# Attention with two pairs of heads as a couple: the last 64 queries of both scored on four quarters of TensorE

## The chip, the cores and the metric

The kernel runs on one core of a Trainium2 chip. The metric is the device time of one execution in microseconds; before the change the median of three runs is 960.37 us (960.06 to 960.45). Less is better.

## What is computed

Three stages follow each other. The first is causal attention with a gated memory read, the other two are chains of matrix products:

```python
# 4 batches, 8 heads, 576 positions, 64 features a head
scores = q @ k.T / 8; scores = where(causal, -1e9, scores)
a = exp(scores - scores.max(-1)); a /= a.sum(-1) + 1e-9
local = a @ v
q_p = where(q > 0, q, exp(q) - 1) + 1
mem = (q_p @ M_prev) / (q_p . z_prev + 1e-6)
x = g * mem + (1 - g) * local            # g = sigmoid(beta), a number per head
# 2304 tokens of 512 features
x = ((x @ w1) * (x @ w2)) @ w3 @ w_out   # w1, w2: 512 x 1024; w3: 1024 x 1024
h = x @ w_in                             # 512 x 2048
out = (h - tanh(h)) @ moe2_w_out         # 2048 x 512
```

## The kernel before

**The whole.** `block_kernel` runs the attention (to about 220 us, with its last products later), then for six groups of 384 tokens the product of two projections (`ab_pe`, line 846, and `x2_pe`, line 872, to about 550 us), then the tanh stage (`h2_pe`, line 1020, `out_pe`, line 1077). The product w3 @ w_out is formed once by the kernel itself, beside the attention: `fold_pe` (line 303) is a generator of 64 pieces of three matmuls (tile `fo`) that the attention loop takes a few at a time. Weights come as raw 64-bit words and are decoded on chip by `decode` (line 260): for each 128 x 512 block two operations on GpSimd (tiles `T`, `E`), two on ScalarE (`T`, `E`), one on VectorE, then a split in a high part on GpSimd and a low part on VectorE. Names in the trace are tile names: `sc` scores, `st` row maxima and sums, `p` exponentials, `t` transposes in PSUM, `g` transposes copied to SBUF, `o` products with V in PSUM, `xs` the attention result, `r` the q and k of a pair, `v` its V, `mw` and `mo` the memory part, `raw` encoded weights. Every instruction goes through one wrapper, so all have line 50.

**Attention.** Heads are taken two at a time: 16 pairs, four to a batch. A pair's q and k lie in one tile `r`, the first head on partitions 0 to 63, the second on 64 to 127. The 576 queries are blocks u = 0 to 3 of 128 and u = 4 of 64. `GROUPS` (line 390) makes four lots of them: (0, 1), (2), (3), (4); so there are 64 steps m, and the loop at line 770 takes two steps in a round, two rounds to a pair. For a full block, `scores` (line 399) puts the first 64 queries of a head in partitions 0 to 63 of the PSUM tile and the others in 64 to 127, and the two heads in two banks: four matmuls of 64 rows by 64 columns, each with up to 512 moving columns, on the four quarters of the array. For the block of 64 queries the partitions hold the two heads, and 576 keys are cut in two halves of 288, so that only the two quarters on the diagonal are used at a time:

```python
            if us[0][0] == 4:
                for x in range(2):
                    for h, r in hr:
                        y = x ^ h
                        mm(sc[r, y, 0:288], q[r, 512:576], k[r, 288 * y:288 * y + 288], True, y == 0)
```

A bf16 product of `identb` and `maskb` adds the causal mask. Score tiles have two PSUM buffers, transposes two, products two.

**A round.** On each engine the instructions of the attention run in program order (`Ordered`, with `in_order` set). A round at even m does: for the two lots of the round before `recip` (VectorE: reciprocals of the row sums) and `norm` (GpSimd: scaling of `p`); `scores` and `rmax` (VectorE: row maxima) of steps m and m + 1; `work(m)`, that is the background work of the step (`background`, line 710: decoding, memory part) and `exps(m)` (ScalarE); `av` (line 504: one product with V of the pair before, copied out by ScalarE as `xs`); `pieces` of the fold; `trans` (line 473) of the first lot of the round before (TensorE transposes, copied to `g` by ScalarE and VectorE); `work(m + 1)`; more `pieces`; `trans` of the second lot. In the first nine steps `background` comes after `exps` (`SHORT`). `load_qk`, `load_v` and the raw loads are issued from SP; `r` has three buffers, V two, `raw` three. `scale_q` (line 212) multiplies the q of the next pair by 0.125 on ScalarE; it stands at the end of a pair's first round, behind all else.

**After the attention** the order of instructions of the other stages is left to the compiler's scheduler, which also moves the first `ab` products in among the last rounds of the attention.

Of the kernel before, what the change touches and what calls it, by code (L numbers as in the profile page):

```python
# [33 lines left out]
def block_kernel(ctx, tc, qk, qt, vt, mp, zp_d, beta, w1, w2, w3t, wo, wi, wo2, ident_d, mask_d, out):  # L34
# [138 lines left out]
    def tp(o, i):  # L173
# [7 lines left out]
    PIECES = (1, 2, 0, 2)  # L181
# [11 lines left out]
        ("r", RB), ("1", 1), ("2", 2), ("4", 4), ("z", ZB), ("t", TB))]  # L193
# [58 lines left out]
    jobs, todo, raws, live = [], deque(fold_seq), [], [0]  # L252
# [7 lines left out]
    def decode(item):  # L260
        k, raw, dst = item
        late = lambda: fstep[0] >= SHORT
        rb = raw[:].bitcast(U32).rearrange("p (n t) -> p n t", t=2)
        lw, hw = rb[:, :, 0], rb[:, :, 1].bitcast(F32)
        t = apt.tile([128, 512], U32, tag="T", name="T")
# [3 lines left out]
        e = ap2.tile([128, 512], U32, tag="E", name="E")  # L269
# [22 lines left out]
        DV.tensor_tensor(out=lo, in0=tf, in1=hi.bitcast(F32), op=ALU.subtract)  # L292
        if k[0] in range(8):
            folds.append((k, fstep[0]))
# [37 lines left out]
    if True:  # L332
# [57 lines left out]
        GROUPS = ((0, 1), (2,), (3,), (4,))  # L390
        NM = 16 * len(GROUPS)
# [3 lines left out]
        def step(m):  # L395
            P, s = divmod(m, len(GROUPS))
            return P, [(u, 128 * x) for x, u in enumerate(GROUPS[s])]

        def scores(m):
            P, us = step(m)  # L400
            q, k = qk_t[P][:, 0], qk_t[P][:, 1]
            hr = [(h, slice(64 * h, 64 * h + 64)) for h in range(2)]
            sc = sc_t[m] = pss.tile([128, 2, 512], F32, tag="sc", name="sc")
            qs = [(h, r, y, slice(64 * y, 64 * y + 64)) for y in range(2) for h, r in hr]
            for u, a in us:
                if u == 4:
                    continue
# [5 lines left out]
            if us[0][0] == 4:  # L413
                for x in range(2):
# [17 lines left out]
        def exps(m):  # L432
            P, us = step(m)
            st = st_t[m]
            for x, (u, a) in enumerate(us):
                sc = seen(m, u, a)
                p = p_t[P, u] = ap3.tile([128, PW[u]], F32, tag=f"p{u}", name="p")
                p = p[:].rearrange("p (a n) -> p a n", a=2)
# [34 lines left out]
        def trans(P, u):  # L473
            p = p_t.pop((P, u))
            if u == 0:
                g_t[0] = ap2.tile([128, 2, 2, 256], F32, tag="g0", name="g0")
            if u == 2:
                g_t[1] = ap1.tile([128, 4, 2, 320], F32, tag="g1", name="g1")
                g_t[2] = ap1.tile([64, 2, 64], F32, tag="g2", name="g2")
            if u < 4:  # L480
                K = 128 * u + 128
                blocks = [(kb, h) for kb in range(u + 1) for h in range(2)]
                for c in range(0, len(blocks), 4):
# [4 lines left out]
                    G = g_t[0] if u < 2 else g_t[1]  # L488
# [15 lines left out]
        def av(P, grp):  # L504
# [4 lines left out]
            hr = [(h, slice(64 * h, 64 * h + 64)) for h in range(2)]  # L509
# [4 lines left out]
            else:  # L514
                for kb in range(4):
                    q0 = 128 if kb == 3 else 0
                    for h, r in hr:
                        mm(o[r, q0:320], v[:, kb, h], g_t[1][:, kb, h, q0:320], kb == 0, False)
                for h, r in hr:
                    mm(o[r, 256:320], v[0:64, 4, h], g_t[2][:, h], False, True)  # L520
            ch = b * 9 + grp * 4
            finished[0] = 2 * P + grp + 1
# [184 lines left out]
        coming, begun, active, owed = [0], [0], [0], [0]  # L707
        ahead()

        def background(m):  # L710
# [13 lines left out]
            if m >= coming[0] and begun[0] < len(fold_seq) and active[0] < TB:  # L724
# [15 lines left out]
        load_qk(1)  # L740
# [19 lines left out]
        def work(h):  # L760
# [5 lines left out]
            if h < SHORT:  # L766
                background(h)

        m = 0
        while m < NM + 3 or jobs or late or folded[0] < 16 or begun[0] < len(fold_seq):  # L770
            P, s = divmod(m, 4)
            fstep[0] = m
            if 2 <= m <= NM:
                for h in (m - 2, m - 1):
                    recip(h)
                for h in (m - 2, m - 1):
                    norm(h)
            if m < NM:
                fill(FILL["s"].get(m, 0))
                for h in (m, m + 1):  # L780
                    if h == 1:
                        first_q(320, 576)
                    scores(h)
# [3 lines left out]
                if m == 2:  # L787
# [7 lines left out]
            trs = 0 <= m - WAIT < NM  # L795
            pieces(m, PIECES[s])
            if trs:
                fill(FILL["t"].get(m, 0))
                for u in GROUPS[(m - WAIT) % 4]:
                    trans((m - WAIT) // 4, u)  # L800
# [4 lines left out]
            if trs:  # L805
                for u in GROUPS[(m + 1 - WAIT) % 4]:
                    trans((m + 1 - WAIT) // 4, u)
# [383 lines left out]
```

## Time and profile before

| | |
|---|---|
| median of three runs | 960.37 us |
| the profiled execution | 960.0 us, of which the span of instructions is 958.2 us |
| TensorE matmul busy | 942.0 us (98%) |
| TensorE weight load busy | 815.6 us (85%) |
| VectorE | 677.5 us (71%) |
| ScalarE | 621.8 us (65%) |
| GpSimd | 407.0 us (42%) |
| chain that ended last | TensorE 90%, VectorE 6%, ScalarE 2% |

Busy times are unions of the recorded intervals, so overlapping matmuls are not counted twice; the difference of 1.8 us between the execution and its span lies before the first and after the last instruction. An fp32 matmul stands as two records, so that eight `sc` records are four matmuls. The page's averages mix three stages; the change is in the first of them.

### The profile page before, as it was taken

The numbers are of one execution on the slowest core, as the hardware profiler recorded it, in microseconds if no ns is written. First come the engines' busy times: TensorE is split into PE (matmuls) and PEld (weight loads), VectorE is DVE, ScalarE is ACT, GpSimd is POOL, SyncE is SP. The second block draws the span as 40 slices with busy tenths as digits, with TensorE's granted clock in tenths as the row PEclk, the third lists the DMA queues.
The fourth block names the chain that finished last, engine by engine and source line by source line (L and its number), as shares of the span: only waits on it lengthen the run. The fifth ranks groups of instructions, "written<-read, shape, count | busy, mean of one in ns | idle before, by whom it ended". The sixth has DMA issues, their size and how long they took to land.

```text
span 958.2 us, 16304 instructions
## 1 busy us (share of the span) xinstructions
PE 942.0 (98%) x5927; PEld 815.6 (85%) x5928; DVE 677.5 (71%) x1185; ACT 621.8 (65%) x1398; POOL 407.0 (42%) x500
## 2 busy tenths in 40 slices
PE   7999999999999999999999999999999999999998
PEld 3566665668989999999999999999999998999996
DVE  6788877995876653534424678887787888887875
ACT  6788886875456542324526687776777867766864
POOL 5778866884665511202308753222222222222222
PEclk9999999999999999999999999999999999999999
DMA  6454544341445520101501100000000000000000
GB/s 231 174 174 157 187 145 161 120 138 45 143 130 185 170 69 31 55 12 67 155 1 44 45 1 1 1 34 1 20 14 1 34 1 1 34 1 1 34 1 34
DMA packets 26080, 68.29 MB, mean 71 GB/s; under 512 B 4880, under 2 KB 5904, under 8 KB 26000
## 3 DMA queue, kind: packets, MB, share of 16 engines
q1 hardware_dynamic: 25568, 67.12, 21.3%
q8 instruction: 46, 0.75, 0.3%
q14 instruction: 34, 0.28, 0.1%
q10 hardware_dynamic: 432, 0.14, 0.1%
HBM read 62.53 MB, written 4.72 MB: 70 GB/s over the span
## 4 chain that ended last, share of the span: by engine, by line
PE 90%; DVE 6%; ACT 2%; issue 1%; DMA 1%; POOL 1%; SPq 0%; DVEq 0%; ACTq 0%; POOLq 0%
PE o L50 25%; PE h L50 21%; PE ab L50 20%; PE x L50 11%; PE sc L50 4%; PE t L50 4%; PE fo L50 4%; DVE st L50 2%; PE mo L50 2%; ACT p L50 1%; DVE g L50 1%; DVE T L50 1%; DVE mst L50 0%; POOL p L50 0%; DMA r<-in_qk 0%
## 5 line engine op out<-in xcount | busy, mean ns | idle before, releaser
L50 POOL TENSOR_TENSOR gl<-s,gh 128x384 fp32r<-128x384 f32 x96 | 99.7, 1038 | 288.3 <-ACT gh L50 275.8
L50 PE MATMUL x<-abh,wf 128*128 128x384 f32 x384 | 107.0, 342 | 1.1 <-ACT abh L50 1.1
L50 ACT ACTIVATE s<-u,pc 128x384 f32<-128x384 f32 x192 | 107.7, 614 | 0.6 <-POOL gl L50 0.6
L50 PE MATMUL ab<-xh,wa 128*128 128x384 f32 x384 | 106.9, 338 | 0.7 <-ACT xh L50 0.6
L50 PE MATMUL ab<-xh,wb 128*128 128x384 f32 x384 | 106.0, 336 | 0.0
L50 DVE SCALAR_TENSOR_TENSOR s<-s,u 128x384 f32<-128x384 f32 x96 | 84.3, 878 | 25.7 <-ACT s L50 24.9
L50 POOL TENSOR_SCALAR p<-p,st 128x128 f32<-128x128 f32 (+2 forms) x144 | 86.0, 616 | 36.4 <-DVE st L50 26.8
L50 ACT ACTIVATE p<-sc,st 128x128 f32<-128x128 f32 (+2 forms) x144 | 78.1, 555 | 29.2 <-DVE st L50 28.3
L50 ACT ACTIVATE u<-u,pc 128x384 f32<-128x384 f32 x96 | 59.4, 619 | 47.1 <-DVE s L50 47.1
L50 DVE TENSOR_TENSOR a<-ab,a 128x384 f32<-128x384 f32 x48 | 26.4, 552 | 73.1 <-PE ab L50 69.7
L50 PEld LDWEIGHTS x<-abh,wf 128*128 128x128 f32 x384 | 70.2, 188 | 5.6 <-issue 3.9
L50 DVE TENSOR_TENSOR t<-h,t 128x384 f32<-128x384 f32 x96 | 53.2, 554 | 28.8 <-ACT t L50 28.3
L50 POOL TENSOR_SCALAR T<-raw 128x512 f32<-128x512 f32 x72 | 56.6, 787 | 39.1 <-DMA raw<-in_wo 11.5
L50 ACT ACTIVATE u<-h 128x384 f32<-128x384 f32 x96 | 46.7, 487 | 40.7 <-PE h L50 40.7
L50 PEld LDWEIGHTS ab<-xh,wa 128*128 128x128 f32 x384 | 70.1, 188 | 2.1 <-ACT xh L50 0.9
L50 POOL TENSOR_SCALAR E<-raw 128x512 f32<-128x512 f32 x72 | 51.1, 710 | 47.2 <-DVE z2p L50 12.8
L50 PEld LDWEIGHTS ab<-xh,wb 128*128 128x128 f32 x384 | 70.0, 188 | 0.3 <-issue 0.3
L50 DVE SCALAR_TENSOR_TENSOR s<-s,s 128x384 f32<-128x384 f32 x96 | 63.9, 665 | 8.7 <-DVE s L50 0.5
L50 PE MATMUL sc<-r 64*64 64x128 f32 (+4 forms) x640 | 64.8, 455 | 0.6 <-DVE r L50 0.6
L50 DVE COPY_PREDICATED s<-u,t 128x384 f32<-128x384 uint32 x96 | 58.7, 612 | 8.9 <-DVE s L50 0.5
L50 PE MATMUL x<-abl,wf 128*128 128x384 f32 x192 | 64.9, 338 | 0.0
L50 ACT ACTIVATE E<-raw 128x512 uint16<-128x512 uint32 x72 | 57.3, 796 | 11.5 <-POOL E L50 11.2
(208 smaller groups left out, 2514.4 us busy)
## 6 DMA issues: line engine op xcount, KB each, us to landing
raw<-in_wo SPq DMA_DIRECT2D x24, 512.0 KB, 3.5
r<-in_qk SPq DMA_DIRECT2D x15, 576.0 KB, 5.1
raw<-in_w3t SPq DMA_DIRECT2D x16, 512.0 KB, 3.8
raw<-in_w SPq DMA_DIRECT2D x16, 512.0 KB, 3.5
raw<-in_wi SPq DMA_DIRECT2D x16, 512.0 KB, 3.6
v<-in_vt SPq DMA_DIRECT2D x16, 320.0 KB, 2.9
mw<-in_qt SPq DMA_DIRECT2D x18, 256.0 KB, 3.8
out<-ob SPq DMA_DIRECT2D x18, 256.0 KB, 2.2
```

Of the source, the lines that this page charges most:

```text
L50: i = call(*args, **kw)
```

## The change

The pairs are taken two at a time (a couple, 2b and 2b + 1), in four rounds of two steps: (0, 1) and (2) of the first pair; (3) of the first and (0, 1) of the second; (2) and (3) of the second; and the last 64 queries of both. In this last round a PSUM tile holds one head, its partitions the two pairs, so that four matmuls of 288 columns run on the four quarters, and both tiles are filled alternately. Each round has one product with V. What was done to both score tiles, exponentials and transposes of the last 64 queries is done as often as before, but each transpose tile is now copied out in two halves, one by ScalarE and one by VectorE, since its halves belong to two pairs. The tile `g1` exists once for each pair of the couple and holds the last 64 keys as well (the tile `g2` goes); `g0`, one of the `E` tiles and two of the four `T` tiles of the decoding are given up or taken from another pool. Each pair's q and k are loaded at the end of the couple's last round, two pairs at a time; pair 1 is loaded before the first raw weights; V is loaded one round before its first use. `scale_q` stands in the middle of the first and third round, between the transposes of the first lot and `work(m + 1)`. In the first nine steps `background` of an even step comes after the transposes of the first lot. `recip`, `norm` and `trans` take the two lots in the same order; in a couple's first round that is the second lot first. The exponentials of a `u = 4` of a second head use the buffer of `p2`.

```diff
-    PIECES = (1, 2, 0, 2)
+    PIECES = (1, 2, 0, 2, 1, 2, 0, 2)
...
-        GROUPS = ((0, 1), (2,), (3,), (4,))
-        NM = 16 * len(GROUPS)
+        SEQ = ((0, (0, 1)), (0, (2,)), (0, (3,)), (1, (0, 1)), (1, (2,)), (1, (3,)), (0, (4,)), (1, (4,)))
+        NM = 64
...
+        def scores_last(m):
+            P, us = step(m)
+            sc = [pss.tile([128, 2, 512], F32, tag="sc", name="sc") for _ in hr]
+            sc_t[m], sc_t[m + 1] = sc
+            for y in range(2):
+                for j, c in hr:
+                    q, k = qk_t[P + j][:, 0], qk_t[P + j][:, 1]
                     for h, r in hr:
-                        y = x ^ h
-                        mm(sc[r, y, 0:288], q[r, 512:576], k[r, 288 * y:288 * y + 288], True, y == 0)
+                        mm(sc[h][c, y, 0:288], q[r, 512:576], k[r, 288 * y:288 * y + 288], True, y == 0)
+            for j, c in hr:
                 for h, r in hr:
-                    mm(sc[r, 1, 224:288], identb[r, r], maskb[r, 0:64], False, True)
+                    mm(sc[h][c, 1, 224:288], identb[r, r], maskb[r, 0:64], False, True)
...
             else:
+                h = P % 2
                 t = psT.tile([128, 4, 128], F32, tag="t", name="t")
                 for kb in range(4):
                     tp(t[:, kb], p[:, 128 * kb:128 * kb + 128])
-                copy(g_t[1][:].rearrange("p a b q -> p (a b) q")[:, :, 256:320],
-                     t[:].rearrange("p a (b q) -> p (a b) q", b=2))
+                for j in range(2):
+                    copy(g_t[1, j][:, :, h, 256:320], t[:, :, 64 * j:64 * j + 64], on_act=j == 0)
                 t = psT.tile([128, 4, 128], F32, tag="t", name="t")
                 tp(t[0:64, 0], p[:, 512:576])
-                copy(g_t[2][:], t[0:64, 0].rearrange("p (b q) -> p b q", b=2), on_act=False)
+                for j in range(2):
+                    copy(g_t[1, j][0:64, 3, h, 0:64], t[0:64, 0, 64 * j:64 * j + 64], on_act=j == 0)
...
+        load_qk(1)
         ahead()
...
+            lots = (m - 2, m - 1) if s else (m - 1, m - 2)
...
+                if s == 6:
+                    scores_last(m)
...
                 if m == 0:
                     set_gates()
-                if m == 2:
                     first_q(0, 576, 1)
             work(m)
             flush_t()
-            if 1 <= P <= 16:
-                av(P - 1, s // 2)
-                if s == 2 and P + 1 < 16:
-                    load_v(P + 1)
+            if s == 0 and 1 <= b <= 8:
+                av(2 * b - 1, 0)
+            if s == 2 and 1 <= b <= 8:
+                av(2 * b - 2, 1)
+                if b < 8:
+                    load_v(2 * b)
+            if s == 4 and b < 8:
+                av(2 * b, 0)
+            if (s == 6 and 1 <= b < 8) or (s == 4 and b == 8):
+                av(2 * b - 1, 1)
+                if b < 8:
+                    load_v(2 * b + 1)
...
+                lot(lots[0])
+            if m < SHORT:
+                background(m)
+            if s == 0 and 1 <= b < 8:
+                scale_q(2 * b + 1)
+            if s == 4 and b < 7:
+                scale_q(2 * b + 2)
             work(m + 1)
...
+                lot(lots[1])
...
-            if s == 0 and 1 <= P <= 16 - RB:
-                load_qk(P + RB - 1)
-            if s == 0 and 1 <= P < 15:
-                scale_q(P + 1)
+            if s == 6:
+                for P in (2 * b + 3, 2 * b + 4):
+                    if P < 16:
+                        load_qk(P)
```

## Rows read from the trace of the kernel before

**Rows 1.** Stretches: length, busy us of PE, PEld, DVE, ACT, POOL, clock, DMA, GB/s.

```profile
0.00:42.00 42.00, 35.20 (x297) 17.62 (x299) 28.53 (x62) 29.07 (x83) 26.86 (x50) 0.96 0.58 201
42.00:215.00 173.00, 170.28 (x1617) 111.93 (x1618) 147.13 (x311) 143.87 (x393) 133.36 (x195) 1.00 0.48 157
...
180.00:200.00 20.00, 19.89 (x183) 13.04 (x177) 19.79 (x37) 16.19 (x48) 17.79 (x23) 1.00 0.38 136
```

**Rows 2.** TensorE, one pair of the middle: start, duration, operation, records.

```profile
129.21 1.09 PE L50 MATMUL sc<-r 64*64 64x512 f32 x8
...
130.17 1.16 PE L50 MATMUL sc<-r 64*64 64x288 f32 x8
...
131.29 2.42 PE L50 MATMUL o<-g,v 128*64 128x320 f32 x20
...
136.51 0.45 PE L50 MATMUL sc<-r 64*64 64x128 f32 x8
...
137.31 0.84 PE L50 MATMUL sc<-r 64*64 64x384 f32 x8
...
138.12 0.87 PE L50 MATMUL o<-g,v 128*64 128x256 f32 x8
138.92 0.97 PE L50 MATMUL fo<-wa,zs 128*128 128x512 f32 x3
139.74 1.03 PE L50 MATMUL t<-ident,p 128*128 128x128 f32 x8
140.53 0.95 PE L50 MATMUL fo<-wb,zs 128*128 128x512 f32 x3
...
142.01 0.71 PE L50 MATMUL t<-ident,p 128*128 128x128 f32 x5
```

**Rows 3.** ScalarE in the same pair; in brackets idle before, and releaser.

```profile
130.43 0.73 ACT L50 ACTIVATE r<-r 128x576 f32<-128x576 f32 x1
131.01 0.68 ACT L50 ACTIVATE T<-T 128x512 f32<-128x512 f32 x1
131.79 0.69 ACT L50 ACTIVATE p<-sc,st 128x512 f32<-128x512 f32 x1
...
138.73 0.37 ACT L50 ACTIVATE p<-sc,st 128x128 f32<-128x128 f32 x1 [1.16 <-DVE st L50]
...
140.33 0.48 ACT L50 ACTIVATE xs<-o,omgt 128x256 f32<-128x256 f32 x1
140.69 0.61 ACT L50 ACTIVATE g<-t 128x512 f32<-128x512 f32 x1
141.17 0.82 ACT L50 ACTIVATE E<-raw 128x512 uint16<-128x512 uint32 x1
141.80 0.60 ACT L50 ACTIVATE p<-sc,st 128x384 f32<-128x384 f32 x1
...
142.35 0.62 ACT L50 ACTIVATE p<-sc,st 128x384 f32<-128x384 f32 x1
```

**Rows 4.** VectorE in the same pair: the row maxima of its second round.

```profile
137.62 1.89 DVE L50 TENSOR_REDUCE st<-sc 128x2 f32<-128x256 f32 x3
```

**Rows 5.** Opening: the first raw loads, GpSimd's first decode, TensorE after a wait.

```profile
2.75 1.55 SPq L50 DMA_DIRECT2D raw<-in_wo  x3
...
9.36 0.64 POOL L50 TENSOR_SCALAR T<-raw 128x512 f32<-128x512 f32 x1 [8.43 <-DMA raw<-in_wo]
...
22.79 0.84 PE L50 MATMUL t<-ident,p 128*128 128x128 f32 x5 [1.62 <-ACT g L50]
23.57 1.98 PE L50 MATMUL sc<-r 64*64 64x512 f32 x8
...
25.42 1.79 PE L50 MATMUL sc<-r 64*64 64x288 f32 x8
```

**Rows 6.** DMA issues from 42 to 215 us: count, size, median us to landing.

```profile
r<-in_qk SPq DMA_DIRECT2D x11, 576.0 KB, 5.1
v<-in_vt SPq DMA_DIRECT2D x13, 320.0 KB, 2.9
```

More of the change, by code (lines that the diff above doesn't have):

```diff
@@ L251, in block_kernel @@
     folds, fstep, folded, fold_open = deque(), [0], [0], [False]
-    jobs, todo, raws, live = [], deque(fold_seq), [], [0]
+    jobs, todo, raws, live, turn, going = [], deque(fold_seq), [], [0], [0], set()
     def ahead():
@@ L264, in decode @@
         lw, hw = rb[:, :, 0], rb[:, :, 1].bitcast(F32)
-        t = apt.tile([128, 512], U32, tag="T", name="T")
+        n = turn[0]
+        turn[0] += 1
+        going.add(n)
+        t = (stg["T"] if n & 2 else apt).tile([128, 512], U32, tag="T", name="T")
         tf = t[:].bitcast(F32)
@@ L268, in decode @@
         yield 0, 0, 0.7
-        e = ap2.tile([128, 512], U32, tag="E", name="E")
+        e = (stg["E"] if n & 1 else ap1).tile([128, 512], U32, tag="E", name="E")
         PO.tensor_scalar(out=e[:].bitcast(F32), in0=hw, scalar1=2.0 ** -100, scalar2=2.0 ** -53,
@@ L292, in decode @@
         DV.tensor_tensor(out=lo, in0=tf, in1=hi.bitcast(F32), op=ALU.subtract)
+        going.discard(n)
         if k[0] in range(8):
@@ L395, in step @@
         def step(m):
-            P, s = divmod(m, len(GROUPS))
-            return P, [(u, 128 * x) for x, u in enumerate(GROUPS[s])]
+            b, s = divmod(m, 8)
+            j, us = SEQ[s]
+            return 2 * b + j, [(u, 128 * x) for x, u in enumerate(us)]
+        hr = [(h, slice(64 * h, 64 * h + 64)) for h in range(2)]
         def scores(m):
@@ L401, in scores @@
             q, k = qk_t[P][:, 0], qk_t[P][:, 1]
-            hr = [(h, slice(64 * h, 64 * h + 64)) for h in range(2)]
             sc = sc_t[m] = pss.tile([128, 2, 512], F32, tag="sc", name="sc")
@@ L436, in exps @@
                 sc = seen(m, u, a)
-                p = p_t[P, u] = ap3.tile([128, PW[u]], F32, tag=f"p{u}", name="p")
-                p = p[:].rearrange("p (a n) -> p a n", a=2)
+                p = p_t[P, u] = ap3.tile([128, PW[u]], F32, tag="p2" if u == 4 and P % 2 else f"p{u}", name="p")
+                p = p[:, 0:576 if u == 4 else PW[u]].rearrange("p (a n) -> p a n", a=2)
                 for h in [slice(0, 1), slice(1, 2)] if u < 4 else [slice(0, 2)]:
@@ L475, in trans @@
             if u == 0:
[L476 removed]
+                g_t[0] = ap1.tile([128, 2, 2, 256], F32, tag="g0", name="g0")
             if u == 2:
[L478 to L479 removed]
+                g_t[1, P % 2] = ap1.tile([128, 4, 2, 320], F32, tag=f"g1{P % 2}", name="g1")
             if u < 4:
@@ L487, in trans @@
                         tp(t[:, m], p[:, K * h + 128 * kb:K * h + 128 * kb + 128])
-                    G = g_t[0] if u < 2 else g_t[1]
+                    G = g_t[0] if u < 2 else g_t[1, P % 2]
                     q0 = 128 * (u % 2)
@@ L508, in av @@
             o = psA.tile([128, 512], F32, tag="o", name="o")
-            hr = [(h, slice(64 * h, 64 * h + 64)) for h in range(2)]
             if grp == 0:
@@ L517, in av @@
                     for h, r in hr:
-                        mm(o[r, q0:320], v[:, kb, h], g_t[1][:, kb, h, q0:320], kb == 0, False)
+                        mm(o[r, q0:320], v[:, kb, h], g_t[1, P % 2][:, kb, h, q0:320], kb == 0, False)
                 for h, r in hr:
-                    mm(o[r, 256:320], v[0:64, 4, h], g_t[2][:, h], False, True)
+                    mm(o[r, 256:320], v[0:64, 4, h], g_t[1, P % 2][0:64, 3, h, 0:64], False, True)
             ch = b * 9 + grp * 4
-            finished[0] = 2 * P + grp + 1
+            if grp:
+                finished[0] = 2 * P + 2
             for X, e0, e1, s in xpart(ch, ch + n // 64):
@@ L723, in background @@
                     advance(j)
-            if m >= coming[0] and begun[0] < len(fold_seq) and active[0] < TB:
+            if m >= coming[0] and begun[0] < len(fold_seq) and active[0] < TB and turn[0] - 4 not in going:
                 k = fold_seq[begun[0]]
@@ L738, in background @@
                     advance(j)
-        load_qk(1)
         load_v(0)
@@ L765, in work, with lot @@
                 exps(h)
-            if h < SHORT:
+            if h % 2 and h < SHORT:
                 background(h)
+        def lot(h):
+            P, us = step(h)
+            for u, _ in us:
+                trans(P, u)
         m = 0
-        while m < NM + 3 or jobs or late or folded[0] < 16 or begun[0] < len(fold_seq):
-            P, s = divmod(m, 4)
+        while m < NM + 5 or jobs or late or folded[0] < 16 or begun[0] < len(fold_seq):
+            b, s = divmod(m, 8)
             fstep[0] = m
+            lots = (m - 2, m - 1) if s else (m - 1, m - 2)
             if 2 <= m <= NM:
-                for h in (m - 2, m - 1):
+                for h in lots:
                     recip(h)
-                for h in (m - 2, m - 1):
+                for h in lots:
                     norm(h)
@@ L782, in block_kernel @@
                         first_q(320, 576)
-                    scores(h)
+                    if s < 6:
+                        scores(h)
                     rmax(h)
```

12 lines of the change are left out of this document (2 added, 10 removed).

## The prediction

> **What bounds the kernel now.** The busy shares by stretch come first. From 42 to 215 us, nearly all of the attention, TensorE is busy 170.28 of 173.00 us; VectorE, ScalarE and GpSimd are at 147, 144 and 133 [rows 1]. So TensorE is short of 2.7 us in 173, and a microsecond of its work saved there is a microsecond, as long as nobody else has become late. The timeline of one pair then shows the blocks end to end: scores of block 3 at 129.21, of the last 64 queries at 130.17, the product with V at 131.29, the next round at 136.51 [rows 2]. Third, ScalarE in the same pair: it stood still for 1.16 us before the first exponential of the second round, waiting for the row maxima of VectorE [rows 3]. That idle time is the slack of the chain scores, maxima, exponentials. The opening to 42 us is different: TensorE is busy 35.2 of 42 us at a mean granted clock of 0.96 [rows 1].
>
> The Trainium skill (Trainium Kernel Development and Optimization, Performance Expectations) warns that matmul busy time is a bad measure, since matmuls overlap, and prefers the weight loads' busy share. Here that is 111.9 of 173 us, 65% [rows 1]; taken as the bound it would say that TensorE is not short and the saving worth nothing. The end-to-end blocks of rows 2 speak against it: the weights of 64 x 64 are short beside 288 to 512 moving columns. What it leaves is the rival of no gain below.
>
> **The last 64 queries.** Before, a pair spends 130.17 to 131.29 = 1.12 us on them [rows 2]: two times two matmuls of 288 columns, and the mask. After, a couple has two times four of them on four quarters. The four-quarter set of 512 columns of block 3 took 129.21 to 130.17 = 0.96 us, mask and all [rows 2], so 576 columns take 0.96 x 576 / 512 = 1.08, about 1.12 us with the change between sets, for two pairs. Saved: 1.12 us a couple. The other end is zero, if quarters with the same rows but different moving data don't run together. Against that stand the products with V: the two heads' matmuls share all 128 rows, move different data, and the twenty records from 131.29 that write 1152 and 64 columns per head last 2.42 us [rows 2], where fp32 at the rate of block 3 (0.96 us for 512 columns) would need 2.28 us for one head alone. I take 1.12. Seven couples lie in the full stretch: **-7.8 us**; the first is in the opening.
>
> **Moved work.** Products with V, transposes, exponentials, maxima and scalings keep their count, and the fold's pieces their pace by step; TensorE pays nothing for the order. Copies of the last transposes double from 32 to 64, at half the size; ScalarE's total stays, VectorE gets some 0.4 us a pair. It has 26 us free in 173 [rows 1], which hides it, except where VectorE itself is full.
>
> **The wait that is new.** The two tiles of the last 64 queries are filled alternately, so the first matmuls need both score buffers; the round before must have finished both its exponentials. Until now the second buffer was needed about a microsecond later. And `scale_q` goes from a place where ScalarE had idle time (130.43, before the maxima were there) to one in front of the second exponentials; it costs 131.01 - 130.43 = 0.58 us [rows 3]. I lay out the third round, with T its first matmul. TensorE: scores of block 2, 137.31 to 138.12 = 0.81, of block 3, 0.96; V 0.80 (138.12 to 138.92); a piece 0.82; eight transposes 0.79; two pieces 1.48 (140.53 to 142.01); six transposes 0.7; ready for the last 64 queries at T + 6.36 [rows 2]. ScalarE: maxima begin at 137.62 - 136.51 = 1.11 and the 768 columns of block 2 take half of 1.89 us [rows 2, 4]; the exponential started 0.16 us after its maxima, so at T + 2.22; two of them, 0.55 apart and 0.62 long, end at 3.39; `xs` 0.36 to 3.75; the copy of the transposes, ready about 3.8, 0.48 to 4.28; `scale_q` to 4.86; `E` 0.63 to 5.49; two exponentials of 512 columns at 0.69, to 6.87 [rows 3]. TensorE waits 0.5 us. Behind the waiting matmul stand V, the pieces and the transposes of the round, all of TensorE's work. Bounds: zero where no decode falls on that step (0.63 less), 1.15 where two do. I take 0.5: 7 x 0.5 = **+3.5 us**. The same sum for the first round has its last exponential end at about T + 7.0 and the second scores of the next round, which need it, at 7.1: nothing, up to 0.6 with a second decode operation. The later rounds' buffers of `p` are each freed by the first lot's transposes, which ScalarE's copy waits for anyway: nothing.
>
> **VectorE's full stretch.** From 180 to 200 us VectorE is busy 19.79 of 20 us [rows 1]; there it paces and cannot be shortened. The 20 us are three quarters of a couple (26.9 us by twice 129.21 to 142.65): 0.8 us of the saving, plus 0.6 for its added copies, less 0.4 already counted as wait: **+1.0 us**, between 0 and 1.4.
>
> **Loads.** V is loaded a round ahead, q and k when the last 64 queries are scored and V's load is issued. By the blocks above that is at about 3.5 us into the last round, and `scale_q` comes some 7 us later. Landing takes 5.1 us for `r` and 2.9 for V [rows 6]: nothing if they overlap; 1.0 us late a couple if the one follows the other.
>
> **Opening.** Pair 1's 576 KB in front of the raw weights delay GpSimd's first decode from 9.36 [rows 5]; at the 201 GB/s of this stretch [rows 1] by 2.9 us. GpSimd normalises only behind its first three decode operations, so the second round starts up to 1.5 us later. On the other side, with `background` behind the first transposes, ScalarE's copies are earlier: TensorE's wait of 1.62 us at 22.79 can go, and with it the half clock behind it. There the sets took 25.42 - 23.57 = 1.85 us where 0.96 is usual, and 1.79 where 1.16 is [rows 2, 5]: 1.5 us at 1.2 rather than 2.4 GHz. Between +1.5 and -3.1; I take the middle, **-0.8 us**.
>
> **Sum.** The profiled execution is 960.0 us. 960.0 - 7.8 + 3.5 + 1.0 - 0.8 = 955.9; the median of the runs is 0.4 higher: **956.3 us**. The stages behind are bound by TensorE's own work and start so much earlier.
>
> **Rivals.** *All of it.* ScalarE's slack holds, the wait does not appear: 960.4 - 7.8 - 0.8, down to -3.1 in the opening, gives 949.5 to 952, about 951.8. For it: decode operations may fall on the even step. Against: the sum above, 0.5 us too long.
>
> *No gain.* The ring from the last exponential over reciprocals, maxima and the next exponentials, not TensorE, sets the round; it keeps its length when TensorE gets faster. For it: ScalarE and VectorE are at 83 and 85% [rows 1], and they wait for each other in a ring. Against: the idle 1.16 us [rows 3] is slack in just this ring. Time 960.4 - 0.8 = 959.6. The Trainium skill (TensorEngine Tiling (Array Packing), Performance Considerations, PSUM Bottleneck) has this as a rule: tiling speeds the matmuls, not the emptying of PSUM, which may become the bound. By rows 2 and 3 it decides from 1.12 us of wait a couple.
>
> *Slower.* The same chain grows past that point: `scale_q` finds its q 1.0 us late on ScalarE in the first round, which shifts exponentials, reciprocals and maxima of the next; and a second decode operation in front of the third round's exponentials makes the 0.5 us 1.15. Together 2.1 us a couple, 1.0 more than saved: 960.4 + 7 x 1.0 - 0.8 + 1.0 = 967.6 us. For it: three loads on one queue. Against: 16 engines share one transfer, and at most one raw decode comes to a round on average.
>
> *It does not run on four quarters* (the zero end above): no saving, the waits stay: 960.4 + 3.5 + 1.0 - 0.8 = 964.1 us.
>
> **How the numbers follow.** The forecast (954 to 958.4) 0.45, all of it 0.20, no gain 0.20, the two slower ones together 0.15. A change of 0.2%, 1.9 us, is about what a measurement of this kernel can tell. Faster: 0.65; same 0.20; slower 0.15. The range 951.0 to 962.0 leaves out the slower cases and the best tail of the full gain, some 2 in 10; the forecast's own is 954 to 958.4.
>
> **What would show it.** Right: one block of `sc` 64x288 of about 1.1 us for each of eight couples, and before most of them 0.3 to 0.8 us in which TensorE waits for ScalarE's `p`; couples of about 26.3 us instead of 26.9; ScalarE's `r` right before `E` and the exponentials, without a wait for DMA; no wait of 1.6 us near 23 us. Wrong: sets of 2.2 us; no wait at all before them; VectorE or ScalarE busy throughout at unchanged rounds; ScalarE waiting for `r`; or an opening later by more than 1.5 us.

## The result, and the profile after

The changed kernel takes 973.31 us (972.97 to 973.88) against 960.21 us: ratio 1.0135, 95% interval 1.0123 to 1.0147. It is slower by 1.35%, where 0.4% faster was forecast, and 11 us above the range. The profiled execution's span grew from 958.2 to 971.2 us. Its page, with the busy shares and the chain that ended last:

```profile
PE 943.6 (97%) x5928; PEld 812.3 (84%) x5928; DVE 677.5 (70%) x1201; ACT 620.4 (64%) x1414; POOL 409.3 (42%) x500
...
PE 81%; DVE 8%; ACT 6%; POOL 2%; issue 2%; DMA 1%; SPq 0%; DVEq 0%; ACTq 0%; POOLq 0%
```

The stretches of [rows 1], in the same columns:

```profile
0.00:42.00 42.00, 31.42 (x280) 16.17 (x282) 28.24 (x63) 26.62 (x78) 21.71 (x45) 0.88 0.58 193
42.00:215.00 173.00, 163.55 (x1548) 103.30 (x1544) 140.61 (x306) 137.00 (x396) 130.34 (x189) 1.00 0.43 146
180.00:200.00 20.00, 19.59 (x156) 12.62 (x153) 18.85 (x37) 15.21 (x40) 16.67 (x24) 1.00 0.39 126
```

From 42 to 215 us TensorE now idles for 9.45 us instead of 2.72, and no other engine is busier: time went into waiting, not into work. To place it, a couple is measured from its first scores (64x128). Couples 2 to 8 run from there to the first product with V of pair 15; these are the two ends in the kernel before, then in the changed one:

```profile
31.55 0.34 PE L50 MATMUL sc<-r 64*64 64x128 f32 x4
...
219.84 0.44 PE L50 MATMUL o<-g,v 128*64 128x256 f32 x2
```

```profile
32.12 0.71 PE L50 MATMUL sc<-r 64*64 64x128 f32 x8
...
228.65 0.44 PE L50 MATMUL o<-g,v 128*64 128x256 f32 x2
```

Couples 2 to 8 take 196.53 us instead of 188.29: +8.2 us. The first couple ends 0.6 us later, and one product with V of 2.42 us [rows 2] less stands in it, so it lost 3.0. That product stands behind the last couple now, which with 0.5 us more brings the last run of the fold's pieces to +11.7 (246.86 for 235.15). That run has 18 records instead of 15, one piece or 0.6 us more. The first matmul into `h` comes at 563.22 instead of 550.22, +13.0; behind it nothing is lost. So three numbers are to be explained: 3.0, 8.2 and some 1.8 us.

The same two stretches by engine (columns as in rows 1), before and after:

```profile
31.55:219.84 188.29, 184.34 (x1752) 120.58 (x1751) 159.14 (x339) 155.03 (x426) 145.22 (x213) 1.00 0.47 154
```

```profile
32.12:228.65 196.53, 184.97 (x1746) 115.98 (x1745) 159.27 (x347) 153.10 (x440) 146.99 (x212) 0.99 0.43 146
```

TensorE's idle time went from 3.95 to 11.56 us, and its busy time, from which over 7 us of matmuls were taken out, did not fall. The block of the last 64 queries shows why: matmuls and weight loads of one couple, the answer to the block at 130.17 [rows 2].

```profile
107.61 1.78 PE L50 MATMUL sc<-r 64*64 64x288 f32 x13
...
109.21 0.42 PE L50 MATMUL sc<-r 64*64 64x288 f32 x3
...
109.59 2.42 PE L50 MATMUL o<-g,v 128*64 128x320 f32 x20
```

```profile
107.60 0.19 PEld L50 LDWEIGHTS sc<-r 64*64 64x64 f32 x2 [0.17 <-issue]
108.43 0.44 PEld L50 LDWEIGHTS sc<-r 64*64 64x64 f32 x11 [0.64 <-ACT p L50]
```

From 107.61 to 109.59 the block lasts 1.98 us for two pairs. The weight loads show what the matmul row hides: two records, which are one matmul, began, and the rest stood until 108.43, waiting for ScalarE's `p`, which frees the second score buffer. From there to 109.59 is 1.16 us. A matmul that has begun counts as busy while the next one waits. Over couples 2 to 8 the blocks last 1.77, 2.00, 1.98, 1.97, 1.11, 1.92 and 1.93 us, together 12.7; without a wait they would be 7 x 1.1 to 1.16, about 7.9. So about 4.8 us of waiting stand in them. The Trainium skill (Trainium Kernel Development and Optimization, Performance Expectations) calls matmul busy time a bad metric; these two rows agree with it, with 0.64 us in one block.

Who releases the visible waits of TensorE in couples 2 to 8 (total us, times, longest), before and after:

```profile
PEld t L50 <- POOL p L50: 2.8, 6, 1.1
...
PEld sc L50 <- ACT p L50: 1.9, 6, 0.4
```

```profile
PEld sc L50 <- ACT p L50: 11.3, 18, 1.1
...
PEld t L50 <- POOL p L50: 6.0, 14, 0.8
```

Scores wait for score buffers (ScalarE's exponentials late) and transposes for GpSimd's scaling. ScalarE in a couple that begins at 114.37, from the end of its first round (to 121.33) into its second, the answer to [rows 3]:

```profile
119.03 0.69 ACT L50 ACTIVATE r<-r 128x576 f32<-128x576 f32 x1
119.60 0.79 ACT L50 ACTIVATE E<-raw 128x512 uint16<-128x512 uint32 x1
120.24 0.58 ACT L50 ACTIVATE p<-sc,st 128x384 f32<-128x384 f32 x1
...
121.33 0.50 ACT L50 ACTIVATE g<-t 128x256 f32<-128x256 f32 x2
...
124.03 0.69 ACT L50 ACTIVATE p<-sc,st 128x512 f32<-128x512 f32 x1 [1.67 <-DVE st L50]
```

And VectorE at the same time:

```profile
119.10 0.55 DVE L50 COPY g<-t 128x256 f32<-128x256 f32 x2 [0.51 <-ACT g L50]
...
121.76 0.55 DVE L50 COPY g<-t 128x256 f32<-128x256 f32 x2 [1.52 <-ACT g L50]
122.23 0.15 DVE L50 TENSOR_SCALAR st<-st 128x4 f32<-128x4 f32 x1
...
122.77 2.15 DVE L50 TENSOR_REDUCE st<-sc 128x2 f32<-128x1024 f32 x3
```

Read them together. The tile of the last transposes, those of the last 64 queries of the couple before, is copied out half by ScalarE, half by VectorE, and VectorE's half waits for ScalarE's. ScalarE's copy stands behind its exponentials, until 121.33. So VectorE stands 1.52 us, the reciprocals and maxima queued behind come that much later (122.77), and ScalarE then waits 1.67 us for these maxima. The two engines work on the same tile, and neither uses what the other makes. Over couples 2 to 8 these waits of VectorE are the line below (total us, times, longest); the waits of the kernel before have no such line.

```profile
DVE g L50 <- ACT g L50: 11.4, 13, 1.5
```

The opening, against [rows 5]; GpSimd's first decode, then TensorE:

```profile
9.60 0.65 POOL L50 TENSOR_SCALAR T<-raw 128x512 f32<-128x512 f32 x1 [8.67 <-DMA raw<-in_wo]
```

```profile
22.36 0.84 PE L50 MATMUL t<-ident,p 128*128 128x128 f32 x6 [0.93 <-ACT g L50]
...
24.81 1.58 PE L50 MATMUL sc<-r 64*64 64x288 f32 x11 [0.98 <-ACT p L50]
...
28.00 1.89 PE L50 MATMUL t<-ident,p 128*128 128x128 f32 x6 [1.08 <-POOL p L50]
30.25 1.94 PE L50 MATMUL t<-ident,p 128*128 128x128 f32 x8 [0.35 <-ACT g L50]
32.12 0.71 PE L50 MATMUL sc<-r 64*64 64x128 f32 x8
...
33.65 1.52 PE L50 MATMUL sc<-r 64*64 64x384 f32 x8
```

Pair 1's queries and keys in front delayed the raw weights by 0.24 us (9.60 for 9.36), not by 2.9. The old stall at 22.79 is smaller (0.93 us at 22.36), but the last-64 round of the first couple has no product with V in it (none is ready), and TensorE stands before and behind its scores. The granted clock is 0.62 from 24 to 28 us and 0.50, which is 1.2 GHz, from 28 to 32 (0.66 and 1.00 before), and six transposes take 1.89 us, where 0.87 is usual; the scores to 35.20 run at half clock too, 1.5 us more than before.

### The profile page after: what moved, and what is told of

It reads as the page before. It is cut to its first block, busy times and chain, and to the rows that moved or that the text cites. A ratio compares the mean times of both kernels' runs of the same rounds, so it can differ in the third digit from the quotient of the medians.

```text
span 971.2 us, 16272 instructions
## 1 busy us (share of the span) xinstructions
PE 943.6 (97%) x5928; PEld 812.3 (84%) x5928; DVE 677.5 (70%) x1201; ACT 620.4 (64%) x1414; POOL 409.3 (42%) x500
## 4 chain that ended last, share of the span: by engine, by line
PE 81%; DVE 8%; ACT 6%; POOL 2%; issue 2%; DMA 1%; SPq 0%; DVEq 0%; ACTq 0%; POOLq 0%
PE o L50 23%; PE h L50 21%; PE ab L50 20%; PE x L50 10%; ACT p L50 3%; DVE st L50 3%; PE t L50 2%; PE fo L50 2%; PE mo L50 2%; POOL p L50 1%; PE sc L50 1%; DVE g L50 1%; ACT E L50 1%; DVE T L50 1%; ACT g L50 1%
## 5 line engine op out<-in xcount | busy, mean ns | idle before, releaser
L50 POOL TENSOR_SCALAR p<-p,st 128x128 f32<-128x128 f32 (+3 forms) x144 | 89.9, 643 | 44.0 <-DVE st L50 42.1
L50 ACT ACTIVATE p<-sc,st 128x128 f32<-128x128 f32 (+3 forms) x144 | 77.6, 553 | 44.0 <-DVE st L50 43.2
L50 PE MATMUL t<-ident,p 128*128 128x128 f32 (+1 forms) x400 | 60.0, 283 | 11.8 <-DVE g L50 3.8
L50 POOL TENSOR_SCALAR T<-raw 128x512 f32<-128x512 f32 x72 | 53.2, 739 | 41.7 <-DVE wa L50 10.4
L50 PE MATMUL sc<-r 64*64 64x128 f32 (+4 forms) x640 | 62.1, 456 | 7.6 <-ACT p L50 4.2
L50 PEld LDWEIGHTS t<-ident,p 128*128 128x128 f32 (+1 forms) x400 | 45.4, 142 | 26.1 <-POOL p L50 10.9
```

The lines of the kernel that those rows point to most:

```text
L50: i = call(*args, **kw)
```

## Experiments

Theory T: TensorE still sets the pace, and the loss is new waits in front of it. Theory R: the ring scores, maxima, exponentials, reciprocals, scaling, transposes sets it, through in-order queues, and a gain of TensorE is given back. The times are medians, each compared with the kernel before on the same chip; "couples" is the length of couples 2 to 8 in the profiled execution (before 188.3, changed 196.5). Gains in the text are differences to the changed kernel's 973.31 us. The kernel before, measured beside each run, lay between 959.46 and 960.21 us, so the gains are uncertain by up to 0.8 us. Counted against the kernel before that ran beside each, a1's gain of 4.2 is 3.4, and a3's 1.5 and a5's 1.4 are 0.7 and 0.6, which is within the intervals. In favour of the larger values, a2 ran on the same chip as these three, had no effect in its trace, and took 973.30.

| kernel | median us | ratio, interval | couples us |
|---|---|---|---|
| a1 copies by one engine | 969.16 | 1.0106 [1.0089, 1.0123] | 193.2 |
| a2 pair by pair | 973.30 | 1.0146 [1.0131, 1.0161] | 196.4 |
| a3 one scaling earlier | 971.84 | 1.0130 [1.0115, 1.0145] | 194.3 |
| a5 exponentials first | 971.96 | 1.0131 [1.0115, 1.0146] | 195.3 |
| b1 first head's tile first | 973.50 | 1.0147 [1.0133, 1.0161] | 196.7 |
| a6 four small edits | 967.61 | 1.0089 [1.0075, 1.0103] | 190.4 |
| c1 later reciprocals | 973.76 | 1.0153 [1.0139, 1.0167] | 196.4 |
| d1 the same, before | 959.20 | 0.9998 [0.9987, 1.0008] | 188.7 |
| e1 old block, new order | 971.89 | 1.0122 [1.0107, 1.0138] | 194.9 |
| e3 block doubled | 979.07 | 1.0191 [1.0177, 1.0205] | 204.3 |
| e3b doubled, before | 966.52 | 1.0068 [1.0055, 1.0081] | 194.2 |
| e6 no scaling in the loop | 970.33 | 1.0100 [1.0085, 1.0115] | 192.3 |
| f1 opening filled | 975.77 | 1.0165 [1.0148, 1.0183] | 196.6 |
| f2 three causes | 966.41 | 1.0061 [1.0048, 1.0074] | 187.7 |
| f3 no normalising | 970.02 | 1.0104 [1.0090, 1.0117] | 193.6 |
| f3b the same, before | 959.83 | 0.9997 [0.9988, 1.0005] | 188.3 |
| g1 V product first | 977.18 | 1.0179 [1.0165, 1.0193] | 200.1 |
| g2 the same on a6 | 974.57 | 1.0155 [1.0141, 1.0169] | 197.1 |

**The copies (a1).**

```diff
-copy(g_t[1, j][:, :, h, 256:320], t[..], on_act=j == 0)
+copy(g_t[1, j][:, :, h, 256:320], t[..])
-copy(g_t[1, j][0:64, 3, h, 0:64], t[..], on_act=j == 0)
+copy(g_t[1, j][0:64, 3, h, 0:64], t[..], on_act=False)
```

> The kernel after, but the two halves of a transpose tile of the last 64 queries are copied out by one engine: the large tile by ScalarE, the small one by VectorE. In the program of the kernel after, VectorE's half waits on ScalarE's semaphore (both read the same PSUM tile), and in the trace VectorE stood 0.51 and 1.52 us before these copies until ScalarE's half was done. Theory C (this wait lengthens the ring copies, reciprocals, maxima, exponentials): 0.8 us at the end of each couple's first round, 7 couples, so 4 to 6 us less than the kernel after. Rival S (the ring has slack there and the loss sits in the other waits): within 1 us of the kernel after.

It gave 4.2 us back, 3.3 of it in the couples. VectorE in the same place of its couple (which begins at 112.46):

```profile
118.36 0.35 DVE L50 COPY g<-t 64x64 f32<-64x64 f32 x2 [0.47 <-PE t L50]
118.63 0.53 DVE L50 TENSOR_SCALAR st<-st 128x4 f32<-128x4 f32 x1
```

The reciprocals begin 6.17 us into the couple instead of 122.23 - 114.37 = 7.86, and the wait for ScalarE is gone. So the split copies cost 3.4 to 4.2 us.

**The scaling of q (a3, e6).** a3 puts the scaling of the next even pair into the round before, ahead of the exponentials:

```diff
+if s == 2 and b < 7:
+    scale_q(2 * b + 2)
 work(m)
...
-if s == 4 and b < 7:
-    scale_q(2 * b + 2)
```

> The kernel after, but the scaling of the even pair's q moves from the third round, in front of the exponentials that the last 64 queries wait for, to the second round ahead of its first exponentials, where ScalarE stood idle 1.67 us until the maxima came. The odd pair's scaling stays. Theory W (the wait of the second matmul of the last 64 queries, 0.82 us at 107.61, is ScalarE's queue, of which the scaling is 0.58): 0.58 x 7 = 4 us less. Theory R (ring): 2 to 4 us less too, but the wait before the last 64 queries goes while others grow. Rival (the wait is only moved): within 1 us.

e6 takes both scalings out:

```diff
-if s == 0 and 1 <= b < 8:
-    scale_q(2 * b + 1)
-if s == 4 and b < 7:
-    scale_q(2 * b + 2)
```

> The changed kernel without the scaling of q in the loop (the queries of pairs 2 to 15 stay unscaled, so this part of the computation is left out; their number and size of matmuls stay). If the place of the scaling costs only what moving half of it earlier gave, 1.5 to 3 us: 970 to 972 us. If ScalarE's queue is in the ring that paces the couples, each of the 14 scalings takes some 0.6 us of it: 964 to 967 us.

a3 gave 1.5 us. Its blocks of the last 64 last 1.21, 1.42, 1.41, 1.39, 1.11, 1.66 and 1.94 us, together 2.5 less than before the edit, and the couples of that execution 2.2 less: there, most of what was taken from the wait is paid out. e6 gave 3.0 us, nearer to the smaller size. Its profile is of an execution 1.5 us under its median: 4.3 us in the couples, of which 1.8 are in the blocks, so that the scalings seem to cost elsewhere too. No run took the scalings out of the kernel before; how much of the 3.0 us is due to their new place is not shown.

**The order inside ScalarE's queue and the fill (a5, b1, a2).** a5 puts the exponentials of odd steps ahead of the decode; b1 (second diff) fills the first head's tile before the second; a2 (third) fills pair by pair:

```diff
-if h >= SHORT: background(h)
+if h >= SHORT and not h % 2: background(h)
 if h < NM: exps(h)
-if h % 2 and h < SHORT: background(h)
+if h % 2: background(h)
```

```diff
-for y in range(2):
-    for j, c in hr:
-        ...
-        for h, r in hr:
+for h, r in hr:
+    for y in range(2):
+        for j, c in hr:
 ...
```

```diff
-for y in range(2):
-    for j, c in hr:
-        ...
+for j, c in hr:
+    ...
+    for y in range(2):
         for h, r in hr:
```

> The kernel after, but in the odd steps the exponentials stand ahead of the background work (a decode operation of 0.65 us on ScalarE and others on GpSimd and VectorE). If ScalarE's queue in front of the second exponentials is what TensorE's score matmuls and the ring wait for (theories W and R), 0.65 us a round in some 28 rounds can go: 5 to 13 us less than the kernel after. If the loss sits in the copies, GpSimd or the opening: within 2 us; later decoding may cost up to 3 us more.

> The kernel after, but the matmuls of the last 64 queries fill the first head's tile and then the second's, two quarters at a time. TensorE has the same 1.1 us a couple more as in the run with two quarters (which cost nothing), but the first tile no longer needs the second score buffer, so its maxima no longer wait for the exponentials of the step before (VectorE stood 0.82 us at 137.50 in the kernel after). Theory R (the ring over exponentials, scores, maxima sets the round): 0.8 us x 7 = 4 to 7 us less than the kernel after. Theory W (only the order of buffers on TensorE counts): 1.1 us a couple of matmuls against 0.8 us of wait, within 2 us of the kernel after.

> The kernel after, but the matmuls of the last 64 queries run over one pair and then the other, so that two quarters work at a time as before the change; nothing else differs. Theory T (TensorE still sets the round, the other losses stand beside its saving): 1.1 us a couple more, 8 to 9 us more than the kernel after. Theory R (the ring over ScalarE, VectorE and GpSimd sets the round, and TensorE's saving is given back as waiting): within 2 us of the kernel after.

a5 gave 1.4 us, below what was expected of it; b1 and a2 nothing. Six of b1's blocks stayed at 1.76 to 1.99 us (the fifth took 1.40, for 1.11). a2 did not undo the quarters: its middle block took 1.99 us (107.25 to 109.24) and its fifth, without the wait, 1.18, where the old block takes 2.17 (e1 below), so it tells nothing of their worth.

**Four edits together (a6).** a1, a3, a5, and the opening's decode in the old order:

```diff
-if h % 2: background(h)
+if h % 2 or h < SHORT: background(h)
...
-if m < SHORT: background(m)
```

> The kernel after with four edits at once: a transpose tile of the last 64 queries is copied out by one engine, the even pair's scaling stands in the second round ahead of its exponentials, the exponentials of odd steps stand ahead of their background work, and the background work of the first nine steps stands where the kernel before has it. Alone, the first three gave 4.2, 1.5 and 1.4 us. Theory R (each shortens one ring, so they add up): 7 to 9 us less than the kernel after, some 965 us. Rival (after the first of them another chain, GpSimd's scaling or the transposes, sets the round): 4 to 5 us less.

967.6 us, 5.7 less; singly a1, a3 and a5 sum to 7.0. In five of the seven couples its block has no wait (the other two take 1.77 and 1.61 us):

```profile
103.82 1.20 PE L50 MATMUL sc<-r 64*64 64x288 f32 x16
104.84 0.21 PE L50 MATMUL sc<-maskb,identb 64*64 64x64 bf16 x4
104.98 1.30 PE L50 MATMUL o<-g,v 128*64 128x320 f32 x8
```

1.16 us for two pairs; this is what four quarters are worth when nobody is late. It is the best version found that computes the whole, and still slower than before.

**One link of the ring (c1, d1).** The second lot's reciprocals go behind the maxima of the new round:

```diff
-for h in lots: recip(h)
-for h in lots: norm(h)
+recip(lots[0]); norm(lots[0])
 ...
     rmax(h)
+    if h == m and m >= 2: recip(lots[1]); norm(lots[1])
```

> The kernel after, but the reciprocals and the scaling of the second lot stand behind the row maxima of step m instead of ahead of them. So VectorE no longer waits for the last exponentials of the round before it takes the next maxima: the ring exponentials, reciprocals, maxima, exponentials is cut. Theory R: the round falls towards TensorE's own work, 5 to 12 us less than the kernel after, and TensorE's waits for score buffers are what is left. Rival G (GpSimd's scaling and the transposes behind it set the round): scaling comes later, 0 to 5 us more.

> The kernel before with the same edit: reciprocals and scaling of the second lot behind the row maxima of step m. There TensorE's blocks stand end to end, so theory R with a ring just shorter than TensorE's round says little gain: 0 to 3 us less than the kernel before, in the opening and around 180 to 200 us. Rival G: 1 to 4 us more.

No change in either kernel. The reciprocals in front of the maxima alone do not set the pace.

**The quarters undone alone (e1).** The old block, a pair to a tile, in the new order of rounds:

```diff
...
-mm(sc[h][c, y, 0:288], q[r, 512:576], k[r, 288 * y:288 * y + 288], True, y == 0)
+mm(sc[j][r, y, 0:288], q[r, 512:576], k[r, 288 * y:288 * y + 288], True, y == 0)
...
```

> The order of the rounds stays as changed, but the last 64 queries of a pair are again filled on two quarters, each pair into a tile of its own (heads on the two halves of the partitions), and their tiles are copied out as before: the first tile no longer waits for the second buffer, and the copies are one large and one small again. Against the changed kernel with these copies on one engine each (969.2 us): if TensorE still paces the couples, 1.12 us x 8 of matmuls come back and the wait of 0.82 us x 7 goes: 969.2 + 9.0 - 5.7 = 972.4 us. If the chain through ScalarE, VectorE and GpSimd paces them, the longer fill is hidden and only the wait counts or nothing: 963.5 to 969.2 us. If the four quarters are what costs the time, it falls to before, 960 us.

971.9 us, 2.7 above a1 (2.1 counted against the kernels before beside them), which shares its undivided copies: as T said (972.4). Its block:

```profile
107.16 1.19 PE L50 MATMUL sc<-r 64*64 64x288 f32 x8
...
108.20 1.17 PE L50 MATMUL sc<-r 64*64 64x288 f32 x8
...
109.33 1.03 PE L50 MATMUL o<-g,v 128*64 128x320 f32 x6
```

2.17 us and no wait, against 1.98 us with the wait in the changed kernel: in this couple the quarters save 0.19 us, not 1.01. And the new order of rounds, with its buffers and without the quarters, is 11.7 us slower than before. The loss is in the order and what came with it (buffers, loads, opening), not in the quarters. The decoding tiles that were given up don't show as a cause in the couples: GpSimd waited 2.1 us there for a free `T` before, and 0.6 in the changed kernel.

**More TensorE work (e3, e3b).** The scores of the last 64 queries issued twice, and the control:

```diff
-for y in range(2):
+for x in range(4):
+    y = x % 2
...
-mm(.., True, y == 0)
+mm(.., True, x < 3)
```

> The changed kernel, with the score matmuls of the last 64 queries issued twice into the same place (the second time over the first): 8 matmuls of 288 columns more in a couple, on four quarters about 0.96 us of TensorE, 7.7 us in all. If TensorE paces the couples: 973.3 + 7.7 = 981 us. If the ring through ScalarE, VectorE and GpSimd paces them, TensorE has slack there, though the first tile comes later by as much: 973.3 to 976 us.

> The control on the kernel before: the same matmuls doubled, in the odd pairs alone, so that the same 0.96 us x 8 = 7.7 us of TensorE is added. Both theories hold the kernel before to be paced by TensorE here: 959.5 + 7.7 = 967.2 us (965 to 968). If it isn't, and the result stays below 962, the kernel before has slack too and the doubling of the changed kernel says nothing.

+5.8 us in the median, between what T and R said, where 7 x 0.97 was added in the couples; the control, with the same added to the odd pairs, +6.4. (The +7.8 in e3's couples is from an execution of 981.71 us, the slowest of its five.) Most of the work added here is paid, in both kernels. That fits T and speaks against slack of TensorE at this place; but the doubled matmuls also stand in front of their own maxima, so a ring that goes through them would lengthen as well. It doesn't tell the two apart as cleanly as was thought.

**GpSimd's scaling (f3, f3b).** Left out, in both kernels:

```diff
-PO.tensor_scalar(out=pr, in0=pr, scalar1=sc, scalar2=1.0, op0=ALU.mult, op1=ALU.mult)
```

> The changed kernel without GpSimd's scaling of the exponentials by the reciprocal of their sum (this part of the computation is left out). Transposes wait for it 4.8 us in 42 to 215 us, against 1.0 us before. If its lateness is a cause of the loss, the gain here is at least 3 us larger than in the control. If not, both move alike, by 1 to 3 us: 970 to 972 us.

> The control: the kernel before without the same scaling. Transposes waited for GpSimd 1.0 us in 42 to 215 us and in the opening some 1 us more: 957 to 959 us under both theories.

-3.3 us in the changed kernel, -0.1 before. In the old order GpSimd's scaling was hidden; in the new one it costs 3 us. That this is its lateness is likely, not shown: without it GpSimd also has more time for decoding.

**The opening and the sum (f1, f2).** f1's edit is below; f2 is f1 with a1's and e6's edits.

```diff
-FILL = {None: 7, "s": {2: 6}, "t": {2: 3}}
+FILL = {None: 7, "s": {2: 6, 6: 4}, "t": {2: 3, 6: 5}}
...
+dst = spare if m < 6 else psA.tile([128, 512], F32, tag="o", name="spare")
 for _ in range(n):
-    mm(spare, warm[:, 0:128], warm[:, 128:640], True, True)
+    mm(dst, warm[:, 0:128], warm[:, 128:640], True, True)
```

> The changed kernel with 9 matmuls that compute nothing needed (128x512, bf16) in the last round of the first couple: 4 ahead of the last-64 scores, 5 ahead of the transposes, where TensorE idles for 0.98 and 1.08 us and the granted clock is 0.50 to 0.62 from 24 to 36 us. If the fall of the clock is part of the loss, the transposes and scores from 28.0 to 35.2 us run at full clock: the 6 and 8 transposes take 1.94 us instead of 3.83, the three sets of scores 1.95 instead of 3.08, so up to 3.0 us come back: 970.3 us. If these stretches wait for ScalarE and GpSimd anyway, the clock costs nothing: 973.3 us, and 974 if the fill matmuls themselves stand in the way.

> The changed kernel with three things taken away together: each tile of the last 64 queries copied out by one engine, the opening filled as in f1_opening_filled, and the scaling of q in the loop left out (the queries of pairs 2 to 15 stay unscaled). If the causes stand one behind another on TensorE's path they add up: 973.3 - 4.2 - 3.0 - (0 to 3.0) = 963 to 966 us, still slower than before, which means a cause that isn't named yet. If one frees what the other waits for anyway: 966 to 969 us. At 960 us or below the loss is explained.

f1 became 2.5 us slower, but it brought a wait of its own; GpSimd and TensorE in it:

```profile
26.61 0.63 POOL L50 TENSOR_SCALAR T<-raw 128x512 f32<-128x512 f32 x1 [2.65 <-PE spare L50]
```

```profile
29.40 0.33 PE L50 MATMUL t<-ident,p 128*128 128x128 f32 x1 [2.88 <-POOL p L50]
```

A decode now waits for the fill matmuls, whose operand lies in memory that the decode's `T` takes over; GpSimd's scaling behind it and the transposes with it come 1.4 us later. (This profile is of the fastest of five runs that spread from 973.81 to 977.79 us.) The fills held the granted clock at 1.00 from 24 to 28 us, but behind the wait of 2.88 us it fell again, to 0.66 from 32 to 36. So what the clock costs is left open. f2 carries the same flaw; without the fills it might stand 2.5 us lower by f1's loss, an estimate of 964. Its couples are short all the same: 187.7 us, 0.6 under the kernel before, which still has its scalings. Copies (3.3) and scalings (4.3 in the couples) add up: 8.8 together.

**The wait covered (g1, g2).**

```diff
 if s == 6:
+    if 1 <= b < 8:
+        av(2 * b - 1, 1)
+        load_v(2 * b + 1)
     scores_last(m)
...
-if (s == 6 and 1 <= b < 8) or (s == 4 and b == 8):
+if s == 4 and b == 8:
     av(2 * b - 1, 1)
-    if b < 8:
-        load_v(2 * b + 1)
```

> The changed kernel with the V product of the couple's last round put ahead of the scores of the last 64 queries, from behind them, in couples 2 to 8. The scores then wait for both score buffers while TensorE has 2.42 us of matmuls to do. If that wait (0.82 us in the couple that was read) is paid by TensorE in each couple, up to 0.82 x 7 = 5.7 us come back: 967.6 to 970 us. If the maxima and exponentials of the last 64, later by 2.4 us, are what the next round waits for, it is the same or slower: 973 to 978 us.

> The same move on top of the four small edits (967.6 us), where ScalarE's queue is shorter. If the wait is paid: 962 to 965 us. If the later exponentials take its place: 967 to 972 us.

Slower by 3.9 us, and by 7.0 on a6. One couple of g1:

```profile
110.82 1.14 PE L50 MATMUL sc<-r 64*64 64x288 f32 x14
...
112.45 0.77 PE L50 MATMUL t<-ident,p 128*128 128x128 f32 x5 [0.20 <-POOL p L50]
...
114.37 0.63 PE L50 MATMUL t<-ident,p 128*128 128x128 f32 x4 [0.47 <-ACT g L50]
115.88 0.66 PE L50 MATMUL t<-ident,p 128*128 128x128 f32 x4 [0.88 <-DVE g L50]
```

The wait in front of the scores is gone in most couples, and TensorE's busy time in couples 2 to 8 is 4.2 us less (180.80). But its idle time is 19.3 us instead of 11.6. The V product was the work that covered the maxima and exponentials of the last 64 queries; ScalarE's copy of the transposes is queued behind those exponentials, VectorE's come later too, and TensorE now waits there (in the couples 7.9 us until VectorE's copies, for 3.8). Covering one wait uncovered a longer one: here R is right.

## Why the prediction was wrong

The step that failed is **moved work**: "TensorE pays nothing for the order". e1 puts a price of 11.7 us on the new order without the quarters; the quarters take 2.7 off it (a1), and the split copies add 4.2.

*Copies.* "VectorE has 26 us free in 173, which hides it." VectorE did have the time; what cost 4.2 us (a1) was not its length but its place: a copy that waits for another engine's copy, with reciprocals and maxima queued behind it. The prediction asked of each moved step how long it lasts, and not what its engine's queue holds up while it waits. GpSimd's scaling was named in the opening alone and otherwise only counted, and costs 3.3 us in the new order (f3), 0.1 in the old.

*The quarters.* Right in mechanism: 1.16 us for two pairs (1.12 forecast), with no wait. Against the kernel before the saving is 2 x 1.12 - 1.16 = 1.08 us a couple, 7.6 instead of 7.8 (1.01 against e1's block).

*The new wait.* Right in mechanism, place and engine; mis-sized, 4.8 us in seven couples for 3.5. The scaling in front of the exponentials, which the sum carried with 0.58 us, shows: with it left out, e6's middle block is 1.41 us instead of 1.98.

*Opening.* -0.8 forecast, +3.0 measured. The raw loads were nearly harmless, and the stall at 22.79 did shrink. What was missed: the first couple's last round has lost the V product that stood between scores and transposes (27.17 to 29.5 before). That it has none is read from the trace; a run that gives it one was not made.

*VectorE's full stretch.* +1.0 forecast; not visible by itself, and not tested. VectorE is 18.85 of 20 us busy there now.

*Loads.* Nothing forecast, and `r` lands in 5.2 us, V in 2.9, as in [rows 6]. In the waits of 42 to 215 us no scaling is held by a load, so half of the slower rival, a q that comes late, did not happen. Its other half, a chain grown past the saving, did; 967.6 was the nearest of the rivals.

For couples 2 to 8, -3.3 was forecast and +8.2 measured, 11.5 apart. With their waits the seven blocks took 12.7 us where fourteen took 15.7, 3.0 less instead of 4.3: 1.3. With the copies 3.3, GpSimd 2.9 and the half clock at 32 to 35 us 1.5 that makes 9.0, if they add up, which was shown only for copies and the scaling of q. Some 2.5 us there (for which the scalings outside the blocks are a candidate), 1.8 us behind the couples of which one fold piece is 0.6, and what the clock costs in the opening stay without a tested cause. So does the choice between T and R as a whole: added work is mostly paid (e3), and so is a wait shortened at its source (a3), but a covered one comes back elsewhere (g1). That TensorE and the ring are about equally long in this loop would fit all three; it is not shown. The Trainium skill (TensorEngine Tiling (Array Packing), Performance Considerations, PSUM Bottleneck) says that tiling speeds the matmuls and not the emptying of PSUM; the block of 1.98 us, 0.64 of it a wait for ScalarE, agrees.

## What to carry to other kernels

When work is reordered, follow each moved instruction's queue, not its duration: what it waits for, what stands behind it, and who needs that next. Don't split the copy of one tile over two engines without looking at the trace for one half waiting on the other. Where the bounding engine idles only 2% and a ring of other engines may be as long, a saving at one place counts only as far as the next wait, and work between two dependent steps is cover: before moving it, name what will be waited for in its old place.

## What was not expected of the hardware

Eight score matmuls (sixteen records) on four quarters that read two pairs' q and k ran in 1.10 to 1.18 us whenever nothing was late. The first of them, once begun, makes TensorE's row look busy for a wait of 0.64 us that only the weight loads show.
